# A linear-attention and MLP block on Trainium2: small products moved to POOL, query features stored before they are normalized, attention's stages set by steps

## The chip, the cores and the metric

The kernel runs on one core of a Trainium2 chip. The core has five engines that run their own queues in order and wait for each other by semaphores: TensorE (PE in the profile, with PEld for its weight loads), VectorE (DVE), ScalarE (ACT), GpSimd (POOL) and SyncE (SP, which issues most DMAs). The metric is the device time of one execution in microseconds (us); lower is better.

## The reference

One transformer block for 2048 positions of width 1024, in float32:

```
x   = A_x
q, k, v = split(layernorm(x) @ wqkv)             # 32 heads of 32
phi(a)  = [softmax(a @ w_phi), softmax(-a @ w_phi)]   # 64 features per head
num = phi(q) @ (phi(k)^T v)
den = phi(q) @ sum(phi(k)) + 1e-6
h   = x + (num / den) @ wo
out = h + relu(layernorm(h) @ w1) @ w2           # inner width 3584
```

There is no mask: phi(k)^T v and the sum of phi(k) run over all positions, so no query can be finished before all keys have been seen.

## The kernel before

All large products are done three times with operands split into a high and a low part (L180 to L182, one line each), which keeps float32 accuracy. w_phi is folded into the projection weights beforehand. Positions are 16 tiles of 128.

An *item* is one projection of one tile onto 512 columns: 8 groups of three matmuls. The program is a list of items; after group k of item n it runs whatever the table `at[n, k]` holds, and `when(step, f)` puts f at item step // 8, group step % 8. So a *step* is one group of three matmuls, and the table, not a scheduler, sets the order in which every engine's queue receives its instructions. Weights come through six raw buffers and are split by ACT (L124) and by DVE or POOL (L127).

The items run in these stages:

1. keys and values of tiles 0 to 7 (32 items), then queries of these tiles (16 items, the first query half);
2. keys and values of tiles 8 to 15 (32), then their queries (16, the second query half);
3. the output projection (32 items), then the MLP (Strassen-like, seven products per pair of blocks).

**Queries.** At an item's end `q_first` empties the projection bank with four DVE instructions: maximum and minimum of each head (L475, L476), and the two differences into a feature buffer `qe` (L478, L479; three buffers). `q_second` takes the exponential on ACT (L484), `q_third` sums each of the 32 softmaxes and inverts the sums on DVE (L488, L489), `q_fourth` multiplies on POOL (L493), and `q_store` writes the buffer to DRAM from SP (L496, into `ed`). While the first query half runs, the x tiles 8 to 15 are normalized and transposed for the second round of keys (L215, L224 to L226, L232, L239, L176, L177).

**Attention.** It works in 32 *units*, each two tiles and a quarter of the heads. `at_load` reads the unit's features back (L507, four buffers), `at_sums` multiplies them with the summed key features `zb` on POOL (L513, one `ez` buffer), `at_norm` sums on DVE to 16 denominators, adds 1e-6 and inverts (L519, L521, L522), `at_scale` multiplies on POOL (L527), `at_turn` transposes on DVE (L533), `at_num` is 64 small matmuls into four PSUM banks (L546; two of the banks are the `tp` banks that transposes also use), which ACT copies out (L552) and DVE turns into low parts (`at_low`, L561). The first eight units run beside the second query half, one for each 4/3 items, the others at one per item, mostly beside the output projection. `z_sum` makes `zb` (L453).

**Second layer norm.** `ln_pair` works beside the output projections, one pair of tiles each 32 steps: statistics on DVE, three small POOL instructions, ACT, then transposes on PE (L239, L609) through the `tp` banks, which ACT (L241) and DVE (L610, L611) empty.

Of the kernel before, what the change touches and what calls it, by code (L numbers as in the profile page):

```python
# [9 lines left out]
F32 = mybir.dt.float32  # L10
# [57 lines left out]
class Units:  # L68
# [35 lines left out]
    def advance(self, n):  # L104
# [7 lines left out]
        while self.done < self.loaded:  # L112
# [12 lines left out]
            odd = key[0] == "a" or (key[0] in ("kv", "w1") or ring is self.far) and self.done % 2  # L125
# [13 lines left out]
def kernel(  # L139
# [243 lines left out]
    e_of, v_of, phi_of, kv_ps, kd_of, sm_of = {}, {}, {}, {}, {}, {}  # L383
# [87 lines left out]
    def q_first(s, t, ps):  # L471
# [5 lines left out]
        e = pqp.tile([P, 16, 2, 32], F32, name="qe", bufs=3)  # L477
# [3 lines left out]
        sm_of[s, t] = pqp.tile([P, 32], F32, name="qsm", bufs=3)  # L481

    def q_second(s, t):
        act.activation(e_of[s, t], e_of[s, t], AF.Exp)  # L484

    def q_third(s, t):
        sm = sm_of[s, t]
        v.tensor_reduce(out=sm, in_=e_of[s, t].rearrange("p h s f -> p (h s) f"), op=ALU.add, axis=AX.X)  # L488
        v.reciprocal(sm, sm)  # L489

    def q_fourth(s, t):
        e = e_of[s, t].rearrange("p h s f -> p (h s) f")
        pool.tensor_tensor(out=e, in0=e, in1=sm_of.pop((s, t))[:, :, None].to_broadcast([P, 32, 32]), op=ALU.mult)  # L493

    def q_store(s, t):
        sp.dma_start(ed[t][s], e_of.pop((s, t)).rearrange("p h s f -> p (h s f)"))  # L496


    e_q, ez_of, den_of, ph_of, acc_of, phT_of = {}, {}, {}, {}, {}, {}
# [17 lines left out]
    def at_norm(u):  # L517
        den = ap_.tile([P, 16], F32, name="qden", bufs=2)
        v.tensor_reduce(out=den, in_=ez_of.pop(u).rearrange("p i (h x) -> p (i h) x", x=2 * DH),  # L519
                        op=ALU.add, axis=AX.X)  # L520
        v.tensor_scalar_add(den, den, DEN_EPS)  # L521
        v.reciprocal(den, den)  # L522
        den_of[u] = den

    def at_scale(u):
        e = e_q.pop(u).rearrange("p h s f -> p h (s f)")
        pool.tensor_tensor(out=e, in0=e, in1=den_of.pop(u)[:, :, None].to_broadcast([P, 16, 2 * DH]), op=ALU.mult)  # L527
        ph_of[u] = e.rearrange("p h (s f) -> p (h s) f", s=2)
# [301 lines left out]
    def to_half():  # L830
        nonlocal zb, kvL
# [4 lines left out]
        kvL = zk.tile([P, 16, P], F32, name="kvL")  # L836

# [37 lines left out]
    zb = kvL = ap_ = hp = mp = dp = None  # L875
# [172 lines left out]
```

## Time and profile before

| | |
|---|---|
| time, median of 3 runs | 2041.54 us (2037.99 to 2042.43) |
| the profiled execution | 2041.96 us, of which the span 2040.1 us |
| TensorE busy | 1963.6 us of the span (96%) |
| DVE, POOL, ACT busy | 1046.2, 1009.4, 761.5 us |
| TensorE's granted clock, mean | 0.981 |
| POOL's q_fourth (L493) | 32 runs, median 1916 ns |
| DVE's addition of 1e-6 (L521) | 32 runs, 174 to 7243 ns, median 614 |

The time before is set against the profiled execution's: its span is the time from the first to the last recorded instruction. In the tables by window the columns are busy microseconds of each engine with instruction counts, then the granted clock, the share of the DMA engines and GB/s. In timelines a row is start, duration, engine, line, operation and tiles; the bracket is the idle time before it and what ended it.

### The profile page before, as it was taken

How to read it: one execution, taken by the hardware profiler on the slowest of the kernel's cores; microseconds unless marked ns; L12 is line 12 of the kernel's file. 1: busy time of each engine (PE TensorE's matmuls, PEld its weight loads, DVE VectorE, ACT ScalarE, POOL GpSimd, SP SyncE). 2: the span in 40 equal slices, each digit the busy share in tenths (PEclk: the TensorE clock that was granted, in tenths of full speed). 3: DMA queues.
4: the chain of work that ended last, by engine and by line, in shares of the span. 5: the costliest groups of instructions: out<-in, count | busy, mean ns of one | idle time of the engine just before them, and what ended most of it. 6: DMA issues, size and time to landing. Idle time of an engine off the chain costs nothing.

```text
span 2040.1 us, 35927 instructions
## 1 busy us (share of the span) xinstructions
PE 1963.6 (96%) x13432; PEld 1593.3 (78%) x13432; DVE 1046.2 (51%) x1718; ACT 761.5 (37%) x1374; POOL 1009.4 (49%) x879
## 2 busy tenths in 40 slices
PE   6999998999998799999999999999999999999999
PEld 4888876777776677778888887888888888888887
DVE  4655567766678856634555446434443333333333
ACT  4433323322222211213554545444444444444442
POOL 2665686877777765622333322222234444444443
PEclk8999999999999899999999999999999999999999
DMA  4767677655544446576777788656666777876775
GB/s 152 235 213 224 202 229 250 227 178 159 166 145 156 161 140 204 178 233 202 233 242 251 234 276 257 215 180 186 212 226 211 219 213 213 257 236 212 216 215 178
DMA packets 287566, 425.10 MB, mean 208 GB/s; under 512 B 27168, under 2 KB 136736, under 8 KB 287392
## 3 DMA queue, kind: packets, MB, share of 16 engines
q1 hardware_dynamic: 267232, 393.44, 61.5%
q10 hardware_dynamic: 20160, 29.37, 4.0%
q8 instruction: 105, 1.72, 0.3%
q14 instruction: 69, 0.57, 0.1%
HBM read 285.34 MB, written 137.36 MB: 207 GB/s over the span
## 4 chain that ended last, share of the span: by engine, by line
PE 76%; issue 2%; DVE 2%; DMA 2%; POOL 1%; ACT 1%; SPq 0%; ACTq 0%; DVEq 0%; POOLq 0%
PE mm L180 19%; PE mm L182 18%; PE mm L181 18%; PE ac L180 3%; PE ac L182 3%; PE ac L181 3%; PE tp L180 2%; PE tp L181 2%; PE tp L182 2%; PE tp L546 1%; PE ac L546 1%; DMA hT<-hs 1%; DMA ed<-qe 1%; PE tp L239 1%; PE ac L427 0%
## 5 line engine op out<-in xcount | busy, mean ns | idle before, releaser
L127 POOL TENSOR_TENSOR w<-raw,w 128x512 fp32r<-128x512 f32 x364 | 487.5, 1341 | 747.4 <-ACT w L124 693.4
L124 ACT ACTIVATE w<-raw 128x512 fp32r<-128x512 f32 x686 | 409.8, 626 | 515.3 <-PE mm L182 276.8
L127 DVE TENSOR_TENSOR w<-raw,w 128x512 fp32r<-128x512 f32 x322 | 258.6, 803 | 533.7 <-ACT w L124 528.6
L180 PE MATMUL mm<-w,xT 128*128 128x512 f32 x768 | 321.0, 418 | 0.0
L181 PE MATMUL mm<-w,xT 128*128 128x512 f32 x768 | 308.6, 402 | 5.4 <-POOL w L127 3.5
L182 PE MATMUL mm<-w,xT 128*128 128x512 f32 x768 | 308.0, 401 | 0.0
L180 PE MATMUL mm<-hT,w 128*128 128x512 f32 x672 | 266.2, 396 | 4.0 <-DVE c L663 2.2
L182 PE MATMUL mm<-hT,w 128*128 128x512 f32 x672 | 263.1, 392 | 0.0
L181 PE MATMUL mm<-hT,w 128*128 128x512 f32 x672 | 261.4, 389 | 0.0
L181 PEld LDWEIGHTS mm<-w,xT 128*128 128x128 f32 x768 | 147.6, 192 | 38.9 <-POOL w L127 7.3
L180 PEld LDWEIGHTS mm<-w,xT 128*128 128x128 f32 x768 | 147.6, 192 | 34.9 <-issue 1.3
L182 PEld LDWEIGHTS mm<-w,xT 128*128 128x128 f32 x768 | 147.0, 191 | 35.4
L180 PE MATMUL mm<-w 128*128 128x512 f32 x392 | 152.5, 389 | 0.0
L182 PE MATMUL mm<-w 128*128 128x512 f32 x392 | 152.5, 389 | 0.0
L181 PE MATMUL mm<-w 128*128 128x512 f32 x392 | 152.5, 389 | 0.0
L180 PEld LDWEIGHTS mm<-hT,w 128*128 128x128 f32 x672 | 126.3, 188 | 31.6 <-ACT c L660 2.7
L182 PEld LDWEIGHTS mm<-hT,w 128*128 128x128 f32 x672 | 126.2, 188 | 29.3
L181 PEld LDWEIGHTS mm<-hT,w 128*128 128x128 f32 x672 | 126.2, 188 | 27.2
L329 POOL TENSOR_TENSOR b<-b 128x256 f32<-128x256 f32 x112 | 89.5, 800 | 27.7 <-DMA b<-in_w_dram 21.2
L416 POOL TENSOR_TENSOR zacc<-zacc,kphi 128x512 f32<-128x512 f32 x60 | 79.5, 1325 | 43.6 <-DVE kphi L408 43.6
L513 POOL TENSOR_TENSOR ez<-qe,zb 128x1024 f32<-128x1024 f32 x32 | 76.7, 2396 | 45.6 <-DVE qden L519 30.9
L329 POOL TENSOR_TENSOR b<-b,b 128x256 f32<-128x256 f32 x112 | 87.8, 784 | 15.5 <-DMA b<-in_w_dram 9.3
(138 smaller groups left out, 3361.5 us busy)
## 6 DMA issues: line engine op xcount, KB each, us to landing
raw<-t SPq DMA_DIRECT2D x224, 256.0 KB, 3.7
raw<-ad SPq DMA_DIRECT2D x196, 256.0 KB, 3.0
raw<-in_w_dram SPq DMA_DIRECT2D x168, 256.0 KB, 3.0
b<-in_w_dram SPq DMA_DIRECT2D x112, 256.0 KB, 3.2
t<-b SPq DMA_DIRECT2D x112, 256.0 KB, 3.7
ad<-c ACTq DMA_DIRECT2D x84, 256.0 KB, 2.6
ad<-s SPq DMA_DIRECT2D x84, 256.0 KB, 3.8
ed<-qe SPq DMA_DIRECT2D x32, 512.0 KB, 4.0
```

Of the source, the lines that this page charges most:

```text
L124: nc.scalar.activation(w[:, 0, :], raw[1], AF.Copy)
L127: eng.tensor_tensor(out=w[:, 1, :], in0=raw[1], in1=w[:, 0, :].bitcast(F32), op=ALU.subtract)
L180: pe.matmul(ps, a_hi, b_hi, start=first, stop=False, skip_group_check=more)
L181: pe.matmul(ps, a_hi, b_lo, start=False, stop=False, skip_group_check=more)
L182: pe.matmul(ps, a_lo, b_hi, start=False, stop=last, skip_group_check=more)
L239: pe.transpose(pt[:, k, :], xn[:, (4 * j + k) * P:(4 * j + k + 1) * P], ident)
L329: pool.tensor_tensor(out=tsum[j, *out], in0=tsum[j, *a], in1=tsum[j, *b], op=ALU.subtract)
L416: pool.tensor_tensor(out=zacc[s], in0=zacc[s], in1=phi_of[key], op=ALU.add)
L513: pool.tensor_tensor(out=ez, in0=e_q[u].rearrange("p (i h) s f -> p i (h s f)", i=2), in1=zb[:, q, None, :].to_broadcast([P, 2, 512]), op= ...
L546: pe.matmul(banks[g][32 * c:32 * (c + 1), 64 * r:64 * (r + 1)], kvL[rows, 4 * q + 2 * sd + h // 4, 32 * (h % 4):32 * (h % 4 + 1)], phT[row ...
```

## The change

Queries: the exponentials go to DRAM unnormalized, issued by ACT right behind the exponential; the inverted sums of the softmaxes stay in SBUF in a new tile `smq`; `q_fourth` and `q_store` are gone; `qe` has two buffers instead of three. Attention: the sum on DVE now gives 32 values per partition (`qtz`), POOL multiplies them with the inverted softmax sums and adds the two halves of each head (`at_den`), DVE inverts (`at_inverse`), and `at_scale` first makes 32 factors on POOL (`qsd`), then multiplies. The constant 1e-6 is put into `zb`, half in every summed key feature, as a bias of `z_sum`'s copy: a softmax's features sum to 1, so the two of a head give the whole. The stages of a unit stand in a list of steps. The splits of the six weight units in the "far" ring are all on POOL, and the second layer norm's first half starts one step earlier.

```diff
@@ class Units
-            odd = key[0] == "a" or (key[0] in ("kv", "w1") or ring is self.far) and self.done % 2
+            odd = key[0] == "a" or key[0] in ("kv", "w1") and self.done % 2
@@ def z_sum
-        act.activation(zb[:, s, :], pz, AF.Copy)
+        act.activation(zb[:, s, :], pz, AF.Identity, bias=eps)
@@ def q_first
-        e = pqp.tile([P, 16, 2, 32], F32, name="qe", bufs=3)
+        e = pqp.tile([P, 16, 2, 32], F32, name="qe", bufs=2)
...
-        sm_of[s, t] = pqp.tile([P, 32], F32, name="qsm", bufs=3)
     def q_second(s, t):
         act.activation(e_of[s, t], e_of[s, t], AF.Exp)
+        act.dma_start(ed[t][s], e_of[s, t].rearrange("p h s f -> p (h s f)"))
     def q_third(s, t):
-        sm = sm_of[s, t]
-        v.tensor_reduce(out=sm, in_=e_of[s, t].rearrange("p h s f -> p (h s) f"), op=ALU.add, axis=AX.X)
+        sm = smq[:, t, 32 * s:32 * (s + 1)]
+        v.tensor_reduce(out=sm, in_=e_of.pop((s, t)).rearrange("p h s f -> p (h s) f"), op=ALU.add, axis=AX.X)
         v.reciprocal(sm, sm)
-    def q_fourth(s, t):
-        e = e_of[s, t].rearrange("p h s f -> p (h s) f")
-        pool.tensor_tensor(out=e, in0=e, in1=sm_of.pop((s, t))[:, :, None].to_broadcast([P, 32, 32]), op=ALU.mult)
-    def q_store(s, t):
-        sp.dma_start(ed[t][s], e_of.pop((s, t)).rearrange("p h s f -> p (h s f)"))
@@
-    def at_norm(u):
-        den = ap_.tile([P, 16], F32, name="qden", bufs=2)
-        v.tensor_reduce(out=den, in_=ez_of.pop(u).rearrange("p i (h x) -> p (i h) x", x=2 * DH),
-                        op=ALU.add, axis=AX.X)
-        v.tensor_scalar_add(den, den, DEN_EPS)
-        v.reciprocal(den, den)
-        den_of[u] = den
+    def at_reduce(u):
+        tz_of[u] = tz = ap_.tile([P, 32], F32, name="qtz", bufs=2)
+        v.tensor_reduce(out=tz, in_=ez_of.pop(u).rearrange("p i (h f) -> p (i h) f", f=DH), op=ALU.add, axis=AX.X)
+    def sm_half(u):
+        n, q = UNITS[u]
+        return smq[:, 2 * n:2 * n + 2, 16 * q:16 * (q + 1)]
+    def at_den(u):
+        tz = tz_of.pop(u)
+        pool.tensor_tensor(out=tz.rearrange("p (i h) -> p i h", i=2), in0=tz.rearrange("p (i h) -> p i h", i=2),
+                           in1=sm_half(u), op=ALU.mult)
+        tz2 = tz.rearrange("p (h s) -> p h s", s=2)
+        den_of[u] = den = ap_.tile([P, 16], F32, name="qden", bufs=2)
+        pool.tensor_tensor(out=den, in0=tz2[:, :, 0], in1=tz2[:, :, 1], op=ALU.add)
+    def at_inverse(u):
+        v.reciprocal(den_of[u], den_of[u])
     def at_scale(u):
-        e = e_q.pop(u).rearrange("p h s f -> p h (s f)")
-        pool.tensor_tensor(out=e, in0=e, in1=den_of.pop(u)[:, :, None].to_broadcast([P, 16, 2 * DH]), op=ALU.mult)
+        den = den_of.pop(u)
+        sd = ap_.tile([P, 32], F32, name="qsd", bufs=2)
+        pool.tensor_tensor(out=sd.rearrange("p (i h s) -> p i h s", i=2, s=2),
+                           in0=sm_half(u).rearrange("p i (h s) -> p i h s", s=2),
+                           in1=den.rearrange("p (i h) -> p i h", i=2)[:, :, :, None].to_broadcast([P, 2, 8, 2]),
+                           op=ALU.mult)
+        e = e_q.pop(u).rearrange("p h s f -> p (h s) f")
+        pool.tensor_tensor(out=e, in0=e, in1=sd[:, :, None].to_broadcast([P, 32, 32]), op=ALU.mult)
@@ the table of steps
-        when(8 * n + 17, q_third, sl, t)
-        when(8 * n + 20, q_fourth, sl, t)
-        when(8 * n + 25, q_store, sl, t)
+        when(8 * n + 19, q_third, sl, t)
...
-        do(n + 1, 2, at_sums, u)
-        do(n + 1, 7, at_norm, u)
-        do(n + 2, 4, at_scale, u)
-        do(n + 3, 0, at_turn, u)
-        do(n + 3, 5, at_num, u)
-        do(n + 4, 0, at_low, u)
+        for step, f in ((6, at_sums), (10, at_reduce), (13, at_den), (16, at_inverse), (19, at_scale),
+                        (25, at_turn), (30, at_num), (32, at_low)):
+            when(8 * n + step, f, u)
...
-            when(wo0 + 69 + 32 * i + step, ln_pair, 0, i, stage)
+            when(wo0 + 68 + 32 * i + step, ln_pair, 0, i, stage)
```

Beside this there are the tile `smq` (16 tiles x 64 values) and a constant tile `eps` of half of 1e-6, set by POOL.

The order of the instructions moves in three places. **ACT in the second query half**, before (L484 is the exponential, L552 copies a unit's products out of its banks):

```order
L484 ACTIVATE qe<-qe 128x1024
L552 ACTIVATE oT<-tp 128x4x32 x2
L552 ACTIVATE oT<-ac 128x4x32 x2
L484 ACTIVATE qe<-qe 128x1024
L552 ACTIVATE oT<-tp 128x4x32 x2
L552 ACTIVATE oT<-ac 128x4x32 x2
L484 ACTIVATE qe<-qe 128x1024
```

and now (L485, the store L486, and L565 for the copies):

```order
L485 ACTIVATE qe<-qe 128x1024
L486 DMA ed_1_99<-qe 128x1024
L565 ACTIVATE oT<-tp 128x4x32 x2
L565 ACTIVATE oT<-ac 128x4x32 x2
L485 ACTIVATE qe<-qe 128x1024
L486 DMA ed_1_101<-qe 128x1024
L565 ACTIVATE oT<-tp 128x4x32 x2
L565 ACTIVATE oT<-ac 128x4x32 x2
```

Each exponential is followed by its store. Of one item's two entries, the products' copies (step 29 of a unit, group 5) stood ahead of the exponential (step 14, group 6); now both are in group 6 and the exponential with its store stands first.

**POOL in the second query half**, before (L513 is at_sums, L493 q_fourth, L527 at_scale, L127 a weight's split):

```order
L513 TENSOR_TENSOR ez<-qe,zb 128x1024
L127 TENSOR_TENSOR w<-raw,w 128x512
L493 TENSOR_TENSOR qe<-qe,qsm 128x1024
L527 TENSOR_TENSOR qe<-qe,qden 128x1024
L513 TENSOR_TENSOR ez<-qe,zb 128x1024
L493 TENSOR_TENSOR qe<-qe,qsm 128x1024
L527 TENSOR_TENSOR qe<-qe,qden 128x1024
```

and now (L508 is at_sums, L523 and L527 at_den, L535 and L540 at_scale):

```order
L508 TENSOR_TENSOR ez<-qe,zb 128x1024
L535 TENSOR_TENSOR qsd<-smq,qden 128x32
L540 TENSOR_TENSOR qe<-qe,qsd 128x1024
L523 TENSOR_TENSOR qtz<-qtz,smq 128x32
L527 TENSOR_TENSOR qden<-qtz 128x16
L508 TENSOR_TENSOR ez<-qe,zb 128x1024
```

Two large products per unit stay, the one per query item is gone, and three small ones per unit have come; L523 waits for DVE's sum and L535 for DVE's reciprocal.

**PE at the second layer norm**, before (L609 is its last transpose, L546 the products of a unit):

```order
L609 MATMUL tp<-ident,xin 128x128 x4
L180 MATMUL mm<-w,oT 128x512
L181 MATMUL mm<-w,oT 128x512
L182 MATMUL mm<-w,oT 128x512
L546 MATMUL tp<-qe,kvL 32x64 x8
```

and now (L622 and L559):

```order
L622 MATMUL tp<-ident,xin 128x128 x4
L180 MATMUL mm<-w,oT 128x512
L181 MATMUL mm<-w,oT 128x512
L182 MATMUL mm<-w,oT 128x512
L180 MATMUL mm<-w,oT 128x512
L181 MATMUL mm<-w,oT 128x512
L182 MATMUL mm<-w,oT 128x512
L180 MATMUL mm<-w,oT 128x512
L181 MATMUL mm<-w,oT 128x512
L182 MATMUL mm<-w,oT 128x512
L559 MATMUL tp<-qe,kvL 32x64 x8
```

Three groups of matmuls stand between them, where one stood.

More of the change, by code (lines that the diff above doesn't have):

```diff
@@ L830, in to_half @@
     def to_half():
-        nonlocal zb, kvL
+        nonlocal zb, kvL, smq
         folds.close()
@@ L874 @@
     late, wos, late2, late3 = ExitStack(), ExitStack(), ExitStack(), ctx
-    zb = kvL = ap_ = hp = mp = dp = None
+    zb = kvL = smq = ap_ = hp = mp = dp = None
     do(q_n[0, 0], -1, to_half)
```

9 lines of the change are left out of this document (6 added, 3 removed).

## The prediction

> **What bounds the kernel now.** I began with the header, the busy lines and the slices of the profile's page, and cut the span into stages with the table of busy time by window.
>
> ```profile
> span 2040.1 us, 35927 instructions
> PE 1963.6 (96%) x13432; PEld 1593.3 (78%) x13432; DVE 1046.2 (51%) x1718; ACT 761.5 (37%) x1374; POOL 1009.4 (49%) x879
> PEclk8999999999999899999999999999999999999999
> ```
>
> ```profile
> 255.00:378.00 123.00, 110.34 (x502) 86.40 (x501) 88.08 (x145) 44.75 (x59) 94.31 (x105) 0.94 0.71 230
> 326.00:376.00 50.00, 42.49 (x187) 33.40 (x186) 41.21 (x67) 23.10 (x31) 32.85 (x42) 0.90 0.63 206
> 568.00:688.00 120.00, 109.28 (x1445) 86.52 (x1444) 97.38 (x164) 31.07 (x65) 88.83 (x54) 0.94 0.46 149
> 688.00:757.00 69.00, 55.83 (x1067) 44.16 (x1066) 49.28 (x76) 12.17 (x39) 53.19 (x29) 0.88 0.49 161
> 757.00:785.00 28.00, 28.00 (x607) 22.20 (x606) 19.37 (x42) 2.79 (x15) 14.64 (x13) 1.00 0.59 190
> 785.00:910.00 125.00, 113.53 (x2058) 89.75 (x2057) 68.53 (x142) 28.06 (x76) 65.31 (x50) 0.92 0.60 200
> 706.50:720.20 13.70, 8.21 (x142) 6.58 (x143) 9.87 (x19) 0.89 (x4) 4.54 (x3) 0.50 0.63 215
> ```
>
> The columns are the window, its length, then busy time of PE, PEld, DVE, ACT and POOL, and TensorE's granted clock. TensorE is the bound (96%), so only time in which it waits, or runs at a lower clock, can be won. The change touches four stretches: the first query half (255 to 378), the second query half (568 to 688, where attention units begin), the first output projections beside units (688 to 757), and those with the second layer norm (785 to 910). PE stands idle there for 12.66, 10.72, 13.17 and 11.47 us, 48.0 in all. The clock costs beside that: it is granted at 0.50 for a while after a wait, as in the last row. (1 - clock) times the length gives 7.4 + 7.2 + 8.3 + 10.0 = 32.9 us, too much, since part of the half-clock time is idle anyway (in that row PE is busy for 8.21 of 13.70 us, 60%). At 60 to 80% it is 20 to 26 us, about 0.5 us per idle us, so I price **each idle microsecond at 1.5 us**. All four stretches hold some 72 us; the rest of the span is not touched.
>
> Next I asked the list of waits what ended PE's idle time.
>
> ```profile
> PE tp L546 <- issue: 23.2, 10, 6.1
> PE tp L239 <- DVE xT L177: 7.6, 4, 3.7
> PE ac L546 <- issue: 5.1, 3, 2.3
> PE mm L181 <- POOL w L127: 3.5, 4, 1.8
> PE tp L546 <- DVE xin L611: 2.4, 4, 0.6
> ```
>
> "issue" names no releaser, so I read the two largest places in the timelines, DVE and POOL first, PE last.
>
> ```profile
> 698.80 1.22 DVE L519 TENSOR_REDUCE qden<-ez 128x16 f32<-128x1024 f32 x1 [2.05 <-POOL ez L513]
> 700.05 7.24 DVE L521 TENSOR_SCALAR qden<-qden 128x16 f32<-128x16 f32 x1
> 706.00 1.27 POOL L127 TENSOR_TENSOR w<-raw,w 128x512 fp32r<-128x512 f32 x1
> 708.84 1.24 DVE L533 STREAM_TRANSPOSE qe<-qe 128x1024 f32<-128x1024 f32 x1
> 710.17 0.36 PE L546 MATMUL tp<-qe,kvL 32*32 32x64 f32 x8 [6.07 <-issue]
> ```
>
> A DVE scalar add on 16 columns runs for 7.24 us and ends at 707.29, just as POOL's last instruction ends (707.27). The transpose behind it in DVE's queue starts at 708.84, and the products that read it at 710.17, 6.07 us late. The first query half has another cause:
>
> ```profile
> 352.21 0.38 SPq L496 DMA_DIRECT2D ed<-qe  x1
> 359.30 0.69 DVE L478 TENSOR_TENSOR qe<-mm,qmx 128x512 f32<-128x512 f32 x1 [3.82 <-DMA ed<-qe]
> 361.94 0.64 DVE L177 TENSOR_TENSOR xT<-tp,xT 128x512 fp32r<-128x512 f32 x1
> 362.73 1.08 PE L239 MATMUL tp<-ident,xn 128*128 128x128 f32 x4 [3.68 <-DVE xT L177]
> ```
>
> The feature buffer's store is issued late, after POOL's normalization; DVE holds for it, the xT copy behind it frees PE's transpose bank late. Last, five more rows of PE's timeline, the last two from the layer-norm stretch:
>
> ```profile
> 663.49 0.26 PE L546 MATMUL tp<-qe,kvL 32*32 32x64 f32 x1 [2.60 <-issue]
> ...
> 713.83 0.46 PE L546 MATMUL ac<-qe,kvL 32*32 32x64 f32 x13 [1.81 <-issue]
> ...
> 755.65 0.32 PE L546 MATMUL ac<-qe,kvL 32*32 32x64 f32 x10 [0.94 <-issue]
> ...
> 793.12 0.26 PE L546 MATMUL tp<-qe,kvL 32*32 32x64 f32 x4 [0.60 <-DVE xin L611]
> 796.43 0.34 PE L546 MATMUL tp<-qe,kvL 32*32 32x64 f32 x5 [2.17 <-issue]
> ```
>
> The wait of 0.60 us is for a bank that the layer norm still holds. The other four fall inside a unit's products, after the first of them have run; nothing on DVE, POOL or a DMA answers to them.
>
> **The change part by part.** These rows, from the queries on tiles and lines and from the page, price it (ns min/median/max in the first five):
>
> ```profile
> L493 POOL TENSOR_TENSOR qe<-qe,qsm x32: 1906/1916/2367, 273.3 to 711.6; 128x1024 f32<-128x1024 f32 x32
> L521 DVE TENSOR_SCALAR qden<-qden x32: 174/614/7243, 597.8 to 886.6; 128x16 f32<-128x16 f32 x32
> L224 POOL TENSOR_SCALAR sc<-mv x32: 221/223/599, 6.6 to 1156.8; 128x1 f32<-128x1 f32 x32
> L225 POOL TENSOR_TENSOR sc<-sc,half x32: 567/567/992, 7.0 to 1157.4; 128x1 f32<-128x1 f32 x32
> L675 ACTq DMA_DIRECT2D ad<-c x84: 326/326/353, 977.3 to 1499.3; - x84
> L329 POOL TENSOR_TENSOR b<-b 128x256 f32<-128x256 f32 x112 | 89.5, 800 | 27.7 <-DMA b<-in_w_dram 21.2
> L416 POOL TENSOR_TENSOR zacc<-zacc,kphi 128x512 f32<-128x512 f32 x60 | 79.5, 1325 | 43.6 <-DVE kphi L408 43.6
> ```
>
> *POOL.* q_fourth goes: 32 x 1.916 = 61.3 us, half in each query half. Three small products per unit come. None like them is in the trace: 128x1 costs 0.223 or 0.567 us, so 3 cost 0.7 to 1.7. By the slope from 256 to 512 columns (0.525 us) 32 columns cost 0.800 - 224/256 x 0.525 = 0.34; I take 1.0 us per unit, 33 us in all (21 to 54). POOL has per unit 2.4 + 1.9 + 1.0 = 5.3 us against some 7.2 us of TensorE (24 big matmuls and the small ones), so it stays below the bound. If it did not, each unit would pay the excess. Three of the six far splits move from DVE to POOL (about 1.3 us each) at a place where POOL loses four q_fourths: nothing.
>
> *DVE.* L521 goes, 32 x 0.614 us or more, and with it the one instruction that could run for 7.24 us; the sums over 32 columns and the reciprocal cost as before. New is that POOL's small products wait for a sum on DVE, and DVE's reciprocal waits for POOL. Queued behind the reciprocal are the next transpose and, in the query half, the four instructions that empty a projection bank; queued behind POOL's wait are the next unit's product and the weight splits. The steps leave three (2 us) for each handover, so I charge it only in the residuals below.
>
> The Trainium skill (SBUF — State Buffer, Who interferes with whom) says that a DVE tensor_scalar can take a port pair that GpSimd shares and then wait out whole GpSimd instructions, and that a reduction never does. The 7.24 us row agrees. By that rule the 6.07 us halt is L521's own and goes with it, as in the sum below; if the row were a chance event that the next small instruction can meet, 6.07 x 1.5 = 9 us would stay, and the sum would be 2016.6.
>
> *The store.* It moves from SP, behind POOL, to ACT, behind the exponential. It takes 0.33 us of ACT's queue and, with the gap, some 0.4; 32 x 0.4 = 13 us, beside an engine that is busy for 37%. Behind it stand the evictions of a unit's products. SP no longer waits there in front of weight loads. With two feature buffers instead of three, DVE meets the store of the query item two before:
>
> ```profile
> 282.02 1.06 ACT L484 ACTIVATE qe<-qe 128x1024 f32<-128x1024 f32 x1 [4.93 <-DVE qe L479]
> 291.52 0.68 DVE L478 TENSOR_TENSOR qe<-mm,qmx 128x512 f32<-128x512 f32 x1
> DMA to landing us min/median/max: 2.6/4.0/7.0
> ```
>
> From the exponential's end (283.08) to the overwrite two items on is 8.4 us, less 0.4 for the issue: 8.0 us, where the stores took 4.0 us to land, 7.0 at worst. So this wait should vanish too. Where DVE waits longer, its own next copy is late, as before.
>
> *Steps.* The products come one step later and the layer norm one earlier, so three groups of matmuls, not one, lie between its last transpose and the products. That is 2.1 us for DVE to free the bank, where 0.6 us lacked.
>
> *The rest.* The constant in z_sum's bias and one memset are within 0.3 us, before or beside other work.
>
> **The sum, against the profiled execution.** First query half: of 12.66 us idle, 8.5 go; not all, because from 326 to 376 DVE is itself busy for 41.21 of 50 us and TensorE needs about as much. 8.5 x 1.5 = 12.7. Second query half and first projections: 10.72 + 13.17 = 23.9 us, less 5.4 in the three halts inside products shown above (2.60 + 1.81 + 0.94, the kind of the 2.17 row; the order of PE's instructions is the same but for one step, so I leave them), less 5.0 for new handovers: 13.5 x 1.5 = 20.3. Layer-norm stretch: of 2.4 us for L611 1.0 goes, as a sum that waits for its load can still delay DVE there; 1.5. Together 34.5 us. The execution took 2041.96 us (1.9 outside the span), 0.4 above the runs' median of 2041.54, which changes nothing: 2041.96 - 34.5 = **2007.5 us**. Its own range is 1997 to 2018: residuals at zero give 10 us more, doubled 10 less.
>
> **The rivals.** (1) *DVE stays the follower's bound.* In the first query half it is full, and in the second, with 97.38 of 120 us, nearly; then the removed waits reappear as DVE lateness. For it speaks the 326 to 376 row; against it that much of DVE's idle time is POOL's and the store's. Half of the gain then stays: 2041.96 - 17.2 = **2025**. Chance 0.20.
> (2) *It doesn't do what it says for attention*: the halts called "issue" are not DVE's lateness, and only the first half gains: 2041.96 - 12.7 = **2029**. The 7.24 us row speaks against it for the largest. 0.08.
> (3) *Two buffers are too few, slower.* ACT's queue is in order and its store waits its turn; from 8.0 us to landing on, DVE waits in every query item. At 10 us that is 2 us in 30 items, 60 us, of which TensorE's slack of four banks hides little in the first half (15 items, 30 us x 1.5 = 45) and the gain of attention is halved: 2041.96 + 45 - 11 = 2076; at 9 us, 2053. I put **2060**, slower. Against it the longest landing in the trace, 7.0 us. 0.07.
> (4) *All halts go.* The page counts the loads of PE's instructions:
>
> ```profile
> q8 instruction: 105, 1.72, 0.3%
> ```
>
> The halts inside products total 5.4 + 9.1 us (11.47 of the last stretch less 2.4). If they too come from the old order, 14.5 x 1.5 = 22 us more go: **1986**. That each stands amid ready inputs speaks against it. 0.07.
> The Trainium skill (Runtime: NRT & Kernel Launch, Instruction fetch mechanics) says that instructions come in blocks of 16 KiB, fetched ahead and mostly hidden. 1.72 MB in 105 pieces agrees in size; by its "hidden" the halts would be no fetches, which is this rival, and by the 2.17 us row they may be.
>
> **How the numbers follow.** The forecast has 0.58. Likeliest 2007.5; the range from **1995** to **2034** leaves out rival 4, rival 3 and the tails. A measurement of this kernel tells no change within 0.2%, 4.1 us: 2037.5 to 2045.6. Forecast, rivals 1, 2 and 4 are faster but for their edges: **faster 0.87**, **same 0.05**, **slower 0.08**.
>
> **What would show it.** The wait of DVE's feature copy for ed<-qe gone or under 2 us in all; PE's waits for xT below 3 us; no DVE instruction over 1.6 us in attention; PE L546's counterpart waiting under 14 us for "issue", nearly all of it inside products; its wait for the layer norm's copy under 1.5 us; clock 0.97 or more from 568 to 757. Small POOL products over 0.6 us, or long waits of POOL for qtz sums, would make the middle term wrong; stores landing after 8 us the first.

## The result

The changed kernel takes 2003.98 us (median of four runs, 2002.35 to 2005.39), against 2041.28 us for the kernel before: a ratio of 0.982, with a 95% interval of 0.9803 to 0.9837. The forecast was 2007.5 us. The profiled execution took 2005.25 us, 36.7 us less than that of before, where the sum had said 34.5 us. The total is nearly right; its parts are not.

From the page of the changed kernel, header, busy times and granted clock by slice:

```profile
span 2003.5 us, 35992 instructions
PE 1953.1 (97%) x13432; PEld 1581.5 (79%) x13432; DVE 1013.8 (51%) x1683; ACT 764.0 (38%) x1374; POOL 972.7 (49%) x947
PEclk8999999999999999999999999999999999999999
```

The table cuts both profiled executions at the first large matmul of each stage. For each stage: its length, then in brackets TensorE's idle time (gaps over 0.1 us) and the sum of (1 - clock) times length.

| stage, us | before | after | gain | forecast |
|---|---|---|---|---|
| first keys | 239.3 (11.4; 6.8) | 237.3 (9.4; 6.8) | 2.0 | 0 |
| first query half and second keys | 313.0 (12.7; 6.8) | 299.8 (6.1; 0.0) | 13.2 | 12.7 |
| second query half | 120.6 (10.7; 6.8) | 116.9 (5.6; 6.8) | 3.7 | with the next row |
| output projections, items 0 to 7 | 75.9 (13.2; 8.5) | 65.5 (5.5; 3.4) | 10.4 | 20.3 for both |
| output projections, items 8 to 31 (layer norm) | 187.2 (11.5; 10.2) | 176.8 (6.8; 3.4) | 10.4 | 1.5 |
| MLP | 1088.3 (4.0; 0.0) | 1092.4 (3.3; 0.8) | -4.1 | 0 |

The MLP's row is not the change's. Its length in the profiled executions below lies between 1088.3 and 1096.6 us whatever the edit, and is 1094.7 us in one that differs from the kernel before only in how 1e-6 is added. Differences of 4 us in a single profile's total therefore say nothing by themselves; the stages say more.

What ended TensorE's idle time now, with the waits of DVE and POOL that the prediction spoke of, from the list of waits of the changed kernel (total us, times, longest):

```profile
DVE qe L480 <- DMA ed<-qe: 5.1, 2, 4.2
PE tp L239 <- DVE xT L177: 4.0, 3, 1.6
PE tp L239 <- issue: 4.2, 4, 2.0
PE tp L559 <- issue: 3.7, 4, 1.9
PE ac L559 <- issue: 2.7, 2, 2.0
PE mm L180 <- issue: 3.2, 2, 2.3
PE mm L181 <- issue: 2.0, 1, 2.0
PE tp L559 <- POOL qsd L535: 2.1, 1, 2.1
POOL qsd L535 <- DVE qden L530: 26.3, 15, 5.2
POOL qtz L523 <- DVE qtz L514: 14.8, 3, 8.0
POOL ez L508 <- DMA qe<-ed: 23.7, 8, 5.8
ACT xin L232 <- POOL sc L226: 18.7, 6, 6.9
```

The 23.2 us in which the products (L546, now L559) waited for "issue" have become 3.7, and DVE's waits for the feature stores fell from 13.7 us (seven) to 5.1 (two). POOL's waits for DVE's reciprocal and sum (26.3 and 14.8 us) are new. Its wait for a unit's features has grown to 23.7 us in eight places, from this row of the kernel before:

```profile
POOL ez L513 <- DMA qe<-ed: 14.6, 3, 7.1
```

And the layer norm's transposes (L239) now wait 4.2 us, behind a layer-norm activation on ACT (L232) that waits for POOL (18.7 us, where it was 2.2).

The small POOL products and the stores, by tile (ns min/median/max, then us to landing):

```profile
L527 POOL TENSOR_TENSOR qden<-qtz x32: 213/217/220, 581.7 to 843.0; 128x16 f32<-128x16 f32 x32
L535 POOL TENSOR_TENSOR qsd<-smq,qden x32: 244/247/259, 585.4 to 849.8; 128x32 f32<-128x32 f32 x32
DMA to landing us min/median/max: 2.5/4.1/6.8
```

They cost 0.22 to 0.25 us each, 0.71 a unit where 1.0 was charged (32 us in all; the 33 of the prediction is a slip on which nothing rests). The stores land as they did.

### The profile page after: what moved, and what is told of

It reads as the page before. It is cut to its first block, busy times and chain, and to the rows that moved or that the text cites. A ratio compares the mean times of both kernels' runs of the same rounds, so it can differ in the third digit from the quotient of the medians.

```text
span 2003.5 us, 35992 instructions
## 1 busy us (share of the span) xinstructions
PE 1953.1 (97%) x13432; PEld 1581.5 (79%) x13432; DVE 1013.8 (51%) x1683; ACT 764.0 (38%) x1374; POOL 972.7 (49%) x947
## 4 chain that ended last, share of the span: by engine, by line
PE 89%; DMA 4%; POOL 2%; DVE 2%; issue 1%; ACT 1%; SPq 1%; ACTq 0%; POOLq 0%; DVEq 0%
PE mm L180 22%; PE mm L181 22%; PE mm L182 22%; PE ac L182 4%; PE ac L181 4%; PE ac L180 3%; PE tp L181 2%; PE tp L182 2%; PE tp L180 2%; PE tp L239 1%; PE tp L273 1%; POOL w L127 1%; PE tp L559 1%; DMA t<-b 1%; DMA xin<-in_x_dram 1%
## 5 line engine op out<-in xcount | busy, mean ns | idle before, releaser
L127 POOL TENSOR_TENSOR w<-raw,w 128x512 fp32r<-128x512 f32 x364 | 484.8, 1334 | 771.9 <-ACT w L124 721.5
L127 DVE TENSOR_TENSOR w<-raw,w 128x512 fp32r<-128x512 f32 x322 | 257.0, 798 | 537.6 <-ACT w L124 532.6
L329 POOL TENSOR_TENSOR b<-b,b 128x256 f32<-128x256 f32 x112 | 89.6, 800 | 16.7 <-DMA b<-in_w_dram 10.2
L508 POOL TENSOR_TENSOR ez<-qe,zb 128x1024 f32<-128x1024 f32 x32 | 76.5, 2389 | 23.7 <-DMA qe<-ed 23.7
```

Of the source, the lines that this page charges most:

```text
L127: eng.tensor_tensor(out=w[:, 1, :], in0=raw[1], in1=w[:, 0, :].bitcast(F32), op=ALU.subtract)
L329: pool.tensor_tensor(out=tsum[j, *out], in0=tsum[j, *a], in1=tsum[j, *b], op=ALU.subtract)
L508: pool.tensor_tensor(out=ez, in0=e_q[u].rearrange("p (i h) s f -> p i (h s f)", i=2), in1=zb[:, q, None, :].to_broadcast([P, 2, 512]), op= ...
```

## Experiments

Two stories fit the result. The prediction's: each cause that it named was removed, with what it charged. The rival, formed when the two traces were laid side by side: the large gain in the layer-norm stretch comes from the two moved steps, by way of TensorE's supply of instructions, and the addition on DVE (L521) is worth less than its 7.24 us row made it look. The experiments do one part alone, or undo one.

### The two moved steps alone

```diff
-        do(n + 3, 5, at_num, u)
+        do(n + 3, 6, at_num, u)
...
-            when(wo0 + 69 + 32 * i + step, ln_pair, 0, i, stage)
+            when(wo0 + 68 + 32 * i + step, ln_pair, 0, i, stage)
```

> The kernel before, with nothing changed but two entries of the table of steps: a unit's products one step later (29 to 30) and the second layer norm's first half one step earlier (69 to 68). The prediction's theory: this is worth 1.5 us in the layer-norm stretch (the bank is free in time), and the halts inside products stay: 2040. Rival, formed from the two traces: the halts that no engine or transfer answers to are TensorE's supply of instructions, and whether it halts depends on where its blocks of 256 instructions end beside the short products, which the two entries move: the halts in the layer-norm stretch go, about 11 us, and those before it stay or change their size: 2029 to 2032. In the rival's case halts inside the products of units 19, 23 and 27 are gone in this run too.

Measured: 2025.77 us, ratio 0.9912 (0.9891 to 0.9932), 16 us less. The last 24 items of the output projection take 174.2 us (before 187.2): the rival's number and more. The clock answers too. Two windows, of the kernel before, at one of the four layer-norm places (length, busy time by engine, then clock, DMA share and GB/s):

```profile
792.00:796.50 4.50, 1.73 (x115) 1.23 (x118) 3.32 (x5) 0.00 (x0) 3.96 (x3) 0.86 0.01 4
796.50:800.00 3.50, 3.50 (x33) 2.67 (x33) 0.17 (x1) 0.79 (x4) 2.75 (x2) 0.50 0.37 113
```

and the stretch with all four places when only the steps are moved:

```profile
762.00:891.00 129.00, 123.09 (x2498) 98.05 (x2497) 83.62 (x170) 29.44 (x84) 76.73 (x60) 0.99 0.67 217
```

At 792 us TensorE waited 0.60 us for a bank, ran the first products, and then waited 2.17 us (both rows stand in the prediction); the 3.5 us after that ran at half clock. In the second fence the clock is 0.99 over the whole stretch.

What is the 2.17 us wait? The view of DMA traffic of the kernel before, in the half microsecond around its start (794.0 to 794.5), shows nothing but this:

```profile
DMA packets 1, 0.02 MB, mean 33 GB/s; under 512 B 0, under 2 KB 0, under 8 KB 0
q8 instruction: 1, 0.02, 11.8%
```

One packet of instructions. It starts at 794.15 us, TensorE falls idle at 794.26 and resumes at 796.43. The queue q8 fits TensorE: 13432 matmuls and 13432 weight loads make 256 instructions for each of the 105 packets on the page. Nor is this one packet a coincidence. From 568 us on, the kernel before has seven halts of over 0.7 us inside a unit's products or right behind them, and at each of them TensorE resumes 2.2 to 2.8 us after the start of a q8 packet. The long waits for "issue" ahead of a unit's products, such as the 6.07 us, have no such packet. So the halts inside the products are the supply of TensorE's own instructions. That a block is asked for only when the one before is nearly used up is the reading that fits; no run shows it by itself. The Trainium skill (Runtime: NRT & Kernel Launch, Instruction fetch mechanics) has the fetch of a 16 KiB block go on beside execution and calls its cost mostly hidden; in this trace it was not, since a block's packet started here as the last instructions ran out.

### The layer norm's step alone

```diff
-            when(wo0 + 69 + 32 * i + step, ln_pair, 0, i, stage)
+            when(wo0 + 68 + 32 * i + step, ln_pair, 0, i, stage)
```

> The kernel before with only one of the two entries of the first run changed: the second layer norm's first half one step earlier (69 to 68), a unit's products at step 29 as before. Two groups of matmuls now lie between its last transpose and the products of a unit. If that distance decides (the block of instructions that the products need is fetched while the large matmuls run), most of the first run's gain of 13.5 us in that stretch comes with this entry alone: 2027 to 2032. If the products' own step decides, the halts of about 2.2 us at the four layer-norm places stay and only the waits of 0.6 us go: 2036 to 2041.

Measured: 2028.22 us, ratio 0.9939 (0.9924 to 0.9954). This one entry brings 12 of the 16 us, and the last 24 items take 175.7 us. In the list of waits of this run the layer norm's part is down to four waits of a third of a microsecond:

```profile
PE tp L239 <- issue: 1.3, 4, 0.3
```

Three of the four halts are gone; the fourth, behind the last of these units' products, stays (3.33 us here, 2.17 before). The distance decides: with two groups of large matmuls between the last transpose and the products, the bank is free in time, and at the first of the four places a packet of q8 starts at 786.94 us, 2.8 us ahead of the products. With one group the bank came 0.60 us late and the packet 1.9 us after the products had begun. Why the packet starts earlier with the longer distance is not shown.

### DVE's addition, taken out of the kernel before

```diff
-        act.activation(zb[:, s, :], pz, AF.Copy)
+        act.activation(zb[:, s, :], pz, AF.Identity, bias=eps)
...
-        v.tensor_scalar_add(den, den, DEN_EPS)
```

> The kernel before, with the denominators' constant put into zb and DVE's scalar addition (L521) gone, nothing else. The prediction's theory: the addition is what POOL blocks for up to 7.24 us, and the 6.07 us halt behind it goes with it, 6.07 x 1.5 = 9 us: 2032 (2029 to 2035). Rival: the block is POOL's or a chance event and meets the reciprocal that now comes next: a reciprocal on 16 columns then runs for over 2 us and the time stays at 2039 to 2042.

Measured: 2040.48 us, ratio 0.9987 (0.9977 to 0.9998). A gain of 0.4 to 4.7 us, where 9 were expected. The rival that was written down has the time but not the cause, since no reciprocal runs for over 0.26 us. From the timelines of DVE and TensorE at the place of the 6.07 us halt:

```profile
698.97 0.69 DVE L578 TENSOR_TENSOR xh<-mm,xh 128x512 f32<-128x512 f32 x1 [4.37 <-DMA xh<-in_x_dram]
701.71 0.29 PE L545 MATMUL tp<-qe,kvL 32*32 32x64 f32 x9 [2.36 <-issue]
707.56 0.46 PE L545 MATMUL ac<-qe,kvL 32*32 32x64 f32 x13 [4.32 <-issue]
```

(L545 are the products here.) Ahead of this unit's products TensorE now waits 2.36 us and not 6.07. It is not less, because DVE, free of the addition, waits for a load of x, and the transpose that the products read stands behind that in DVE's queue. The halt inside the same products, the row at 713.83 us in the prediction, has grown from 1.81 to 4.32 us. Together that is 6.7 us, where 7.9 were. The run with the moved steps, which still has the addition, shows the second halt at its longest. A window in the idle time there:

```profile
704.50:708.00 3.50, 0.00 (x0) 0.00 (x0) 2.29 (x4) 0.39 (x2) 3.37 (x2) 0.58 0.90 315
```

the DMA queues, all there were in that window, and one of those in the microsecond behind it (packets, MB, share):

```profile
q1 hardware_dynamic: 466, 1.10, 90.3%
...
q8 instruction: 1, 0.02, 5.5%
```

and TensorE's next row in the timeline:

```profile
710.65 0.47 PE L546 MATMUL ac<-qe,kvL 32*32 32x64 f32 x16 [6.16 <-issue]
```

For 3.5 us the data queue fills 90% of the DMA engines and no instruction packet starts; the first starts at 708.24 us, 3.7 us after TensorE stopped, and TensorE resumes at 710.65, 2.4 us later, as at the other halts. Why this packet starts late is not shown. Full DMA engines alone do not do it. In the run with half a block more, further down, a packet started at 778.74 us, 0.2 us before TensorE stopped, and that halt took 1.95 us, though the DMA engines were full:

```profile
777.50:778.90 1.40, 1.40 (x114) 1.16 (x114) 0.88 (x3) 0.00 (x0) 0.00 (x0) 1.00 0.97 335
```

Nor is the 7.24 us row of the kernel before a single event. The run with the layer norm's step alone has one of 7.26 us at the same unit, with the products 5.92 us late:

```profile
L521 DVE TENSOR_SCALAR qden<-qden x32: 174/612/7261, 595.4 to 870.9; 128x16 f32<-128x16 f32 x32
```

In the run with both steps the slowest addition took 1.88 us, and yet TensorE lost 9.1 us at this place (2.9 ahead of the products, 6.16 inside them), against 7.9 in the kernel before. So the long addition comes back in some executions, but it is worth much less than its length: where it is missing, the load of x and then the supply of instructions hold TensorE nearly as long.

### The queries' part alone

```diff
         act.activation(e_of[s, t], e_of[s, t], AF.Exp)
+        act.dma_start(ed[t][s], e_of[s, t].rearrange("p h s f -> p (h s f)"))
...
-        when(8 * n + 20, q_fourth, sl, t)
-        when(8 * n + 25, q_store, sl, t)
```

> The kernel before, with q_fourth and q_store gone and the exponentials written to DRAM by ACT right behind the exponential; three feature buffers and all of attention as before. It leaves out the normalization of the query features. The prediction's theory: the first query half gains 12.7 us (idle from 12.7 to about 4 us, no half-clock time), and the second half gains what POOL's 16 products there delayed, 3 to 8 us: 2021 to 2026. Rival 1 (DVE is full there): half of it, 2035. If the late store is not the cause of the first half's idle time, 2041.

Measured: 2012.71 us, ratio 0.9853 (0.9838 to 0.9868): 29.5 us, more than expected. The first query half gains as forecast (with the second keys 297.4 us, 3.8 idle, full clock):

```profile
254.00:355.00 101.00, 97.56 (x474) 77.42 (x473) 78.52 (x134) 41.62 (x54) 64.30 (x88) 1.00 0.84 278
```

The rest comes from the second query half (8.0 us) and the first eight projections (8.1 us), although attention itself is untouched: its queues lost POOL's 1.9 us products and SP's late stores. With three feature buffers DVE does not wait for a store at all, where the changed kernel, with two, has the 5.1 us above.

### Queries and steps together

The edits of the first and the fourth experiment in one kernel.

> The kernel before with the queries' part (exponentials stored by ACT right behind the exponential, no POOL normalization, three buffers) and the two entries of the steps, and attention's products as before; it leaves out the normalization of the query features. If the two parts add up (29.5 and 16.4 us alone), 1996, which is 8 us under the whole change: then attention's new small products and handovers cost the whole change about that. If they overlap, because both mend the same waits, 2004 or more, and the small products cost nothing.

Measured: 1997.12 us, ratio 0.9794 (0.9776 to 0.9811). Alone the two parts won 29.5 and 16.4 us, together they win 43.4: within the noise they add up. The whole change is 6.9 us slower than this by the medians, though the intervals overlap a little. That is what the rest of it costs: the new attention, without which nothing is normalized, and with it two feature buffers instead of three and the far weights' splits on POOL, which no run takes apart.

### The addition put back into the changed kernel

```diff
     def at_inverse(u):
+        v.tensor_scalar_add(den_of[u], den_of[u], DEN_EPS)
         v.reciprocal(den_of[u], den_of[u])
```

> The changed kernel with DVE's scalar addition of 1e-6 on 16 columns put back in front of the reciprocal, and the constant out of zb. If the addition is blocked by POOL wherever POOL is busy, it runs for 2 to 7 us in some units here too, and the products behind it come late: 2008 to 2016, with additions over 2 us in the trace. If with the new steps and without q_fourth POOL leaves it room, 32 x 0.2 us of DVE time hidden: 2003 to 2006.

Measured: 2009.96 us, ratio 0.9843 (0.9827 to 0.986), 6.0 us above the changed kernel's median, as the first expectation has it, though the two intervals overlap a little. From the tile view (ns min/median/max):

```profile
L530 DVE TENSOR_SCALAR qden<-qden x32: 165/165/2324, 584.9 to 858.0; 128x16 f32<-128x16 f32 x32
```

and from the list of waits:

```profile
POOL qsd L536 <- DVE qden L531: 34.8, 24, 5.0
```

(The constant is out of `zb` in this run.) The addition's median is 165 ns, where it was 614 right behind the sum; it can still be held (over 1.8 us in four units of 32), and POOL's wait for the reciprocal grows from 26.3 to 34.8 us.

### The small products on DVE

```diff
-        pool.tensor_tensor(out=den, in0=tz2[:, :, 0], in1=tz2[:, :, 1], op=ALU.add)
+        v.tensor_tensor(out=den, in0=tz2[:, :, 0], in1=tz2[:, :, 1], op=ALU.add)
...
-        for step, f in ((6, at_sums), (10, at_reduce), (13, at_den), (16, at_inverse), (19, at_scale),
+        for step, f in ((6, at_sums), (10, at_reduce), (10, at_den), (10, at_inverse), (19, at_scale),
```

with the other two products moved in the same way, and the factors made right behind the reciprocal.

> The changed kernel with its three small products of a unit on DVE, right behind the sum over 32 columns and with the reciprocal between them, so that POOL and DVE no longer hand over to each other twice in a unit. If the handovers (POOL's 26.3 us of waits for the reciprocal, 2.1 us of TensorE for the factors) are what the new attention costs, 1996 to 2001. If DVE's own time is scarce there, or POOL blocks its small instructions as it did the scalar addition (single ones over 1 us in the trace), 2005 to 2015.

Measured: 2017.21 us, ratio 0.9888 (0.9873 to 0.9903), 13 us slower than the change. From the tile view:

```profile
L527 DVE TENSOR_TENSOR qden<-qtz x32: 174/2016/2274, 579.6 to 856.4; 128x16 f32<-128x16 f32 x32
```

and from the timelines of DVE and POOL in one unit:

```profile
703.57 0.19 DVE L523 TENSOR_TENSOR qtz<-qtz,smq 128x32 f32<-128x32 f32 x1
703.80 2.27 DVE L527 TENSOR_TENSOR qden<-qtz 128x16 f32<-128x16 f32 x1
...
703.62 2.42 POOL L508 TENSOR_TENSOR ez<-qe,zb 128x1024 f32<-128x1024 f32 x1
```

The addition of 16 columns ends at 706.07 us, with POOL's product (706.04). Of the 32 units 18 hold this addition for 1.8 to 2.3 us and two for 1.2; the other 12, in which no large POOL instruction runs beside it, take 0.17 to 0.18 (the median of 2016 ns lies between the groups). The reason can be read off: there is one `ez` buffer, so DVE's sum releases POOL's next product, which starts at 703.62, between DVE's first and second small instruction. The first slips through (0.19 us), the second meets it. In the kernel before, L521 stood right behind the sum, with 174 ns at best and 614 in the median. The Trainium skill (SBUF — State Buffer, Who interferes with whom) says that a DVE instruction with both inputs in SBUF contends with a GpSimd one that reads SBUF; this run agrees, 2.27 us in the rows above against 0.17. It speaks for the change's choice of POOL for these products.

### Half a block of TensorE instructions more

```diff
+    def filler():
+        pt = tp_bank()
+        for _ in range(32):
+            pe.matmul(pt[0:32, 0:64], ident[0:32, 0:32], ident[0:32, 0:64], start=True, stop=True)
+
+    when(8 * 60 + 3, filler)
```

> The changed kernel with 32 more products of 32 x 64 on TensorE (of the identity, into a free bank, read by nobody) in the middle of the second round of keys, half a block of TensorE's instructions. They cost 0.8 us themselves. If the halts that nothing answers to are the supply of instructions, those at the products of units 0, 5, 9, 14 and 31 leave these units and others appear at other units, two or three units away, and the time moves by up to 8 us either way: 1997 to 2012. If they belong to their places (banks, copies, loads), the same units halt for as long: 2004 to 2006.

Measured: 2009.13 us, ratio 0.985 (0.9836 to 0.9865). The filler cost 3.9 us, not 0.8 (its item grew from 5.59 to 9.47 us), so without it the time is the changed kernel's. But the halts moved. In the changed kernel four of them, from TensorE's timeline:

```profile
596.55 0.79 PE L181 MATMUL mm<-w,xT 128*128 128x512 f32 x1 [1.98 <-issue]
646.23 0.24 PE L559 MATMUL tp<-qe,kvL 32*32 32x64 f32 x2 [1.14 <-issue]
687.77 0.47 PE L559 MATMUL ac<-qe,kvL 32*32 32x64 f32 x16 [1.96 <-issue]
864.32 0.51 PE L180 MATMUL mm<-wf,oT 128*128 128x512 f32 x1 [2.32 <-issue]
```

and with the filler:

```profile
699.59 0.29 PE L559 MATMUL ac<-qe,kvL 32*32 32x64 f32 x2 [1.68 <-issue]
739.62 0.53 PE L181 MATMUL mm<-w,oT 128*128 128x512 f32 x1 [2.92 <-issue]
780.90 0.46 PE L559 MATMUL ac<-qe,kvL 32*32 32x64 f32 x15 [1.95 <-issue]
```

The four stood at items 86, 92, 97 and 119 of the program, these three at items 99, 104 and 109, and of the four places only item 119 keeps a short one (0.86 us). (Ahead of the products of item 97 there is a wait of another kind, during which no packet of q8 starts: 1.88 us in the changed kernel, 3.81 with the filler.) Two shorter halts with the filler, 1.35 and 1.29 us, stand at items 113 and 118. At the four halts of the changed kernel TensorE resumes 2.4 to 2.6 us after the start of a q8 packet, at these three 2.2 to 2.4. Halts that move when 128 instructions are put in 160 us and more ahead of them do not belong to their places. (The filler also takes one turn of the two `tp` banks, so later units have them the other way round; the packets are what speaks for the instructions.) Nor is an offset a cure: it only moved the halts to other units. The second query half gained 6.8 us by it and the last 24 projections lost 6.4.

### Later steps, and loads from ACT

What these 6.9 us over the two parts are was the last question. In the changed kernel POOL stands at the head of its queue for a unit's features, as in the layer-norm stretch at 782 us, with the layer norm's six small instructions and the scaling queued behind:

```profile
782.61 2.39 POOL L508 TENSOR_TENSOR ez<-qe,zb 128x1024 f32<-128x1024 f32 x1 [5.46 <-DMA qe<-ed]
```

The change had moved that product from step 10 to step 6, four groups closer to its load. Three runs:

```diff
-        for step, f in ((6, at_sums), (10, at_reduce), (13, at_den), (16, at_inverse), (19, at_scale),
+        for step, f in ((10, at_sums), (13, at_reduce), (15, at_den), (17, at_inverse), (20, at_scale),
```

> The changed kernel with five of a unit's stages at later steps: the product with zb at 10 (as before the change) in place of 6, its sum at 13, the small products at 15, the reciprocal at 17, the scaling at 20; transposes and products as they are. If the 7 us that the whole change costs over its two parts begin with POOL waiting at the head of its queue for a unit's features (23.7 us in 8 places), with the layer norm's small instructions and the scaling behind it, that wait goes under 8 us, TensorE's waits of 1.6 to 2.0 us for the layer norm's transposes fall to 0.3, and the time is 1996 to 2001. If the shorter way from the product to the scaling makes the products late instead, 2005 to 2012.

> The same, half as far: 8, 11, 14, 17 and 20. By the first theory POOL's wait for the features is halved and the time lies between, 1999 to 2003; by the second, 2003 to 2007.

and, with the steps as they were, the loads on ACT's queue:

```diff
-            sp.dma_start(e[:, 8 * i:8 * (i + 1)].rearrange("p h s f -> p (h s f)"),
+            act.dma_start(e[:, 8 * i:8 * (i + 1)].rearrange("p h s f -> p (h s f)"),
```

> The changed kernel with a unit's two feature loads issued by ACT instead of SP, nothing else. If the loads are late because SP issues them behind the layer norm's four loads and weight loads (2.8 us of issues ahead of one), POOL's wait for them falls from 23.7 to under 12 us and the time to 1998 to 2002. If they are late because a transfer takes 5 to 6 us from its issue to landing whoever issues it, the wait stays at 20 us or more: 2003 to 2006.

Measured: at steps 10 to 20, 1991.09 us, ratio 0.9751 (0.9732 to 0.9769); at 8 to 20, 1995.12 us, 0.9761 (0.9737 to 0.9786); loads on ACT, 1996.16 us, 0.9773 (0.9755 to 0.9792). All three beat the change (0.9803 to 0.9837), and the first is under the 1996 to 2001 that was written. The list of waits of the first:

```profile
POOL ez L508 <- DMA qe<-ed: 6.5, 2, 5.8
PE tp L239 <- issue: 1.3, 4, 0.3
ACT xin L232 <- POOL sc L226: 7.3, 6, 1.5
```

All three rows are the first theory's. POOL's waits for DVE's reciprocal and sum are as long as before in this run (28.9 and 15.0 us), so it was not these handovers that cost the time. The half-way steps lie nearer to the full ones than was expected; their interval does not tell them from the full ones. With the loads on ACT the total wait fell only to 17.9 us, but 11.9 of it is one wait at the start of attention:

```profile
576.07 2.40 POOL L508 TENSOR_TENSOR ez<-qe,zb 128x1024 f32<-128x1024 f32 x1 [11.92 <-DMA qe<-ed]
```

and in the layer-norm stretch seven waits of at most 1.16 us replace the 5.46 and 5.06 us ones, so there the issue behind SP's other loads did count. Both edits together:

> The changed kernel with both of the last edits: a unit's stages at 10, 13, 15, 17 and 20, and its feature loads issued by ACT. If both mend the same thing (POOL held at the head of its queue by a late load, and the layer norm's instructions behind it), there is nothing left for the second: 1990 to 1993. If the loads' issue on ACT has a gain of its own (SP free for the weights), 1983 to 1987. If ACT's issues stand in front of its copies and exponentials where the stages are late anyway, 1994 to 1998.

Measured: 1988.82 us, ratio 0.9752 (0.9735 to 0.977). From 0.9751 this cannot be told apart, as it would be if the two edits mend the same wait. Later steps alone are enough, and at 1991 us they give a kernel that beats both.

## Why the prediction was right, and where it was wrong

**The total** came out 3.5 us from the forecast by the median and 2.2 by the profiled execution, with errors that cancel in part: 6 us too much in the middle, 9 us too little in the layer norm, and about 1 us lost in the stages that were set to zero. That the total came so near is in part luck.

**First query half: right.** 12.7 us were forecast and 13.2 measured, and the queries' part alone brings as much there (15.6 us with three buffers). The cause was the one named, the store behind POOL's product; the two went together, so the runs do not say which of them weighed more. The way there was not exact: idle time fell by 6.6 us, not 8.5, but the half-clock time went altogether (6.8 to 0), so each idle microsecond was worth 2.0. PE's waits for xT are 4.0 us where "below 3" was written, and DVE's for the store 5.1 where "under 2" was.

**Second query half and first projections: right in idle time, wrong in price.** Idle time fell from 23.9 to 11.1 us, 12.8 where 13.5 were forecast; but the gain is 14.1, not 20.3. The step that failed is the price of 1.5 us for each idle microsecond. Over the three terms it holds (24.1 us less idle, 37.7 us gained), but it is an average: the clock falls in pieces, and more of them stayed here. The loss by the clock fell from 15.3 to 10.2 us in this stretch, where it went from 6.8 to nothing in the first query half. The windows of the changed kernel (second query half, first eight projections, the others):

```profile
552.00:669.00 117.00, 111.37 (x1448) 87.29 (x1447) 89.64 (x155) 33.44 (x66) 73.43 (x69) 0.94 0.47 159
669.00:734.00 65.00, 59.52 (x1216) 46.87 (x1215) 36.07 (x72) 11.49 (x41) 55.98 (x55) 0.95 0.54 175
734.00:865.00 131.00, 124.23 (x2499) 98.61 (x2498) 76.69 (x157) 29.66 (x86) 87.72 (x104) 0.99 0.65 210
```

The sign "0.97 or more from 568 to 757" failed with 0.94 and 0.95. The 5.0 us of idle time charged for handovers, 7.5 us at its price, lies near the 6.9 us by which the change is slower than its two parts. That is luck. The run with later steps has handovers as long and gains 23.3 us in this stretch, more than the 20.3 forecast. What cost the time was POOL at the head of its queue for a load that had been given four groups less. This was not foreseen; the prediction read the steps of POOL against DVE but not the step of `at_sums` against its load.

**L521 was over-valued.** The 6.07 us halt was charged to it, as going with it. The block itself comes back (7.24 and 7.26 us in two profiles), but taken out alone the addition brings 0.4 to 4.7 us. The step that failed is that the last wait at this place was taken for the only one: with the addition gone, a load of x and TensorE's instructions end last. The other half of that step, in which the halt stays, was nearer, though not by a second small instruction on DVE. That POOL's large products can block a small DVE instruction is shown again by the small products on DVE, in 20 of 32 units.

**Layer norm: wrong.** 1.5 us forecast, 10.4 measured. The step that failed is "the order of PE's instructions is the same but for one step, so I leave them": the halts inside products were kept as fixed costs. One step earlier for the layer norm took away four bank waits, three of four halts and most of the lost clock (10.2 to 3.4 us); the fourth halt stays (2.17 us before, 2.32 now). Rival 4 had the cause, the old order, and its part in this stretch came true but for that one. The other part did not: 11.6 us of waits for "issue" remain at the products and the matmuls beside them (3.7 + 2.7 + 3.2 + 2.0).

**Two buffers: right.** The landing's longest is 6.8 us against 8.0 available; what DVE still waits costs the first half at most the 2.4 us by which it is longer than in the three-buffer run, and profiles of two-buffer kernels with the same code there differ by as much (297.4 to 299.8 us).

**Small signs.** No DVE instruction of attention ran for over 1.24 us; the small POOL products took 0.22 to 0.25 us; the products' waits for "issue" are 6.4 us, under 14. All as forecast. Long waits of POOL for the qtz sums were named as a sign against the middle term, and they are there (14.8 us); but the run with later steps has them too and reaches that term.

**What stays open.** Why the clock falls after one wait of 2 us and not after another: in the changed kernel it halves after a wait of 1.97 us at 787.54 us,

```profile
786.80:790.22 3.42, 1.45 (x9) 0.96 (x8) 1.58 (x5) 2.71 (x6) 3.17 (x6) 1.00 0.81 229
790.22:793.64 3.42, 3.42 (x13) 2.72 (x12) 2.27 (x3) 1.19 (x2) 3.34 (x4) 0.50 0.24 87
```

and not after one of 1.57 us at 821.56. And why the MLP's length varies by 8 us between profiles of kernels that are the same there. Neither was tried.

## What to carry to other kernels

When TensorE halts amid ready inputs, look at which of its instructions come in a fast burst and at what stands ahead of them: two groups of large matmuls between short transposes and a burst of small products were worth 12 us here, for one number in a table. The length of a blocked instruction is not its price, even when it comes back: ask what ends the next engine's wait once it is gone, here a load and a block of instructions. And when a stage is moved to an earlier step, check it against its load as well as its consumers, since an engine that waits at the head of its queue holds everything behind.

## What the hardware showed that was not expected

- TensorE's instruction packets were not hidden beside short products: TensorE resumed 2.2 to 2.8 us after a packet's start at seven halts of the kernel before, which took 0.9 to 2.6 us. The longest, 6.16 us in another run, had its packet start 3.7 us after the stop.
- Halts on the supply move when 128 TensorE instructions are added 160 us and more ahead of them.
- A DVE tensor_tensor on 16 columns took 1.8 to 2.3 us in 18 of 32 units, where a large POOL product began just before it, and 0.17 to 0.18 in 12 where none ran beside it.
- Small POOL products on 16 and 32 columns took 217 and 247 ns, less than the 0.34 us drawn from the slope of larger ones.
- 32 products of 32 x 64 one after the other into the same rows of a bank took 3.9 us, where the 64 of a unit, spread over four banks, take 1.5.
